# Batch 1's tokens in two transfers, states of batches 2 to 7 in two late groups, batch 3's tokens loaded ahead of batch 0's outputs

## The chip, the cores and the metric

The kernel runs on one core of a Trainium2 chip. The metric is the device time of one execution in microseconds (us). Engines are called as the profile calls them: PE is TensorE, DVE is VectorE, ACT is ScalarE, POOL is GpSimd and SP is SyncE, which here only issues DMAs.

## What is computed

The input has 8 batches of 8 heads, 512 tokens of 64 elements each, and 32 state vectors for each batch and head. Tokens attend to states, states attend to tokens, and the 544 resulting rows of each batch (heads side by side, 512 wide) go through a feed-forward layer with a leaky ReLU.

```python
def _attn_ref(x, state):
    B, H, S, D = x.shape                       # 8, 8, 512, 64; state: 8, 8, 32, 64
    scale = 1.0 / np.sqrt(D)
    a = softmax(scale * np.matmul(x, state.transpose(0, 1, 3, 2)))
    xread = np.matmul(a, state)
    a2 = softmax(scale * np.matmul(state, x.transpose(0, 1, 3, 2)))
    sread = np.matmul(a2, x)
    return np.concatenate([xread, sread], axis=2)

def _moe_ref(x, w_in, w_out):                  # 512x2048 and 2048x512
    h = x @ w_in
    return np.maximum(0.01 * h, h) @ w_out
```

(softmax stands for the reference's lines with maximum, exponential, sum and 1e-9.) Inputs and output are fp32; the kernel multiplies in bf16.

## The kernel before

Since xread @ w_in is a @ (state @ w_in), the kernel forms for each batch M = state @ w_in (`a_m`, in four column blocks c, evicted by `m_evict`) and the hidden layer directly from the probabilities and M (`ff1`, line 378, followed by ACT's Prelu, line 383). The second layer, FF2, is cut into pieces: `piece(b, hT, i, jq)` (line 406) is four matmuls for output tile i of batch b, and four pieces (jq 0 to 3) finish a tile, which `y_store` evicts and sends out through SP's queue.

For each batch the attention part is: tokens are loaded (`load_x`, into a ring of two tiles `xl`), cast to bf16 with heads side by side (`cast_x`, tile `xb`), and transposed, by PE (`a_xt_pe`, `a_xt_full`) or by a DMA on SP's queue (`a_xt_dma`, line 207), into `xT`. `a_scores` (line 236) makes the scores on PE. `a_shift` (three DVE instructions of 128x1024), `a_exp` (ACT) and `a_probs` (DVE) make the token-side probabilities `aT`. `a_max2` (DVE), `a_exp2` (ACT), `a_probs2` (DVE, lines 310 to 315) make the state-side probabilities `a2`; `a_a2t` (line 322) transposes them by a DMA on SP's queue, and `a_sread` (line 330) multiplies them with the tokens into `sr_t`, which a last stage for all states uses.

All orders are written out by hand: each engine runs its instructions in program order, and SP and POOL issue their DMAs in program order. Tile buffers come from rings; PSUM has two banks each for the tags `ph` and `py` and one double bank each for `sc` and `big`.

The prologue (to line 585) loads batch 0 on SP's queue, states of batches 0 and 1 on ACT's, and the weights and tokens of batches 1 and 2 on POOL's queue, with a cast for the weights. `spin` runs matmuls on zeros. The states of batches 2 and 3 come early, as `st2f`, and are turned on PE by `state23`. Then batch 0's hidden layer is made (lines 590 to 633), and from line 637 to 670 FF2 pieces of batch 0 run while batch 1's tokens are transposed and its attention made. Lines 674 to 711 are the hidden layer of batch 1 in 16 steps s, with FF2 pieces between and batch 2's attention; the states of batches 4 to 7 are loaded at step 6 by eight DMAs on SP's queue (`load_state`, line 187). The loop at line 716 does the same for batches 2 to 7: at step 1 of batch b the scores of batch b+1, at step 13 the token transposes of batch b+2; those tokens are loaded at step 0 (`load_x`) and cast by POOL at step 1. Batch 3's tokens are loaded at line 675, cast at line 691 and transposed at line 711. `state_t` (line 192) casts the late states on POOL and transposes them by a DMA on SP's queue.

Of the kernel before, what the change touches and what calls it, by code (L numbers as in the profile page):

```python
# [9 lines left out]
P = 128  # L10
B, H, S, D = 8, 8, 512, 64
NS = 32
# [3 lines left out]
NT = S // P  # L16
# [11 lines left out]
def kernel(  # L28
# [34 lines left out]
    xv = x[0].rearrange("h (p t) d -> p h (t d)", t=NT)  # L63
    for u in range(2):
        nc.sync.dma_start(xf[u][:], xv[:, NK * u:NK * (u + 1)])
    st2f = consts.tile([P, 4, D], FP32, name="st2f")
    nc.sync.dma_start(
        st2f[:], state[2:4].rearrange("b h n d -> (b h n) d").rearrange("(p r) d -> p r d", r=4)
    )
    idle = consts.tile([P, S], BF16, name="idle")  # L70
    nc.vector.memset(idle[:], 0.0)
    warm = consts.tile([P, 2], FP32, name="warm")
# [26 lines left out]
    def load_x(b, eng):  # L99
        xl[b] = xpool.tile([P, H, NT * D], FP32, name="xl", tag="xl", bufs=2)  # L100
        eng.dma_start(xl[b][:], x[b].rearrange("h (p t) d -> p h (t d)", t=NT))
# [4 lines left out]
    def cast_x(b, h0, h1, copy):  # L106
        copy(  # L107
            xs[b][:, :, h0:h1].rearrange("p t h d -> p h t d"),
            xl[b][:, h0:h1].rearrange("p h (t d) -> p h t d", t=NT),
        )  # L110
# [27 lines left out]

    stbd = consts.tile([P, NK, 2, NS], BF16, name="stbd")
    st1 = consts.tile([P, P], BF16, name="st1")  # L140
    st23 = consts.tile([P, 2, P], BF16, name="st23")
    st_t = consts.tile([P, B - 4, P], BF16, name="st_t")
    sr_t = consts.tile([P, NK, B * NS], BF16, name="sr_t")

    stb0 = consts.tile([P, 4, D], BF16, name="stb0")
# [15 lines left out]
            ps[:, :, D:].rearrange("p r (k q) -> p k q r", q=8),  # L161
        )

    stb2 = consts.tile([P, 4, D], BF16, name="stb2")

    def state23():
        ps = psum.tile([P, 4, D], FP32, name="pst2", tag="sc", bufs=1)
        for r in range(4):
            for g in range(2):
                nc.tensor.matmul(  # L170
                    ps[D * g:D * (g + 1), r, :].rearrange("p (c q) -> p c q", q=8),
                    lhsT=stb2[:, r, :],
                    rhs=ident[:].rearrange("p (c v q) -> p c v q", v=2, q=8)[:, :, g],
                    start=True, stop=True,
                )
        SCA(
            st23[:].rearrange("p b (k q r) -> p (b k) q r", k=NK, r=4),
            ps[:].rearrange("p r (c q) -> p c q r", q=8),
        )

    stf = consts.tile([P, B - 4, P], FP32, name="stf")
    stb = consts.tile([P, B - 4, P], BF16, name="stb")

    def load_state():
        for k in range(NK):
            for g in range(2):
                nc.sync.dma_start(
                    stf[NS * k:NS * (k + 1), :, D * g:D * (g + 1)],
                    state[4:, 2 * k + g].rearrange("b n d -> n b d"),
                )  # L190

    def state_t():
        POO(stb[:], stf[:])
        nc.sync.dma_start_transpose(st_t[:], stb[:].rearrange("p b q -> p (b q)"))

# [27 lines left out]
    def st_of(a, g, k):  # L225
        rows = slice(D * g, D * (g + 1))
        if a.b == 0:
            return stbd[rows, k, g ^ (k // 2), :]
        t = st1 if a.b == 1 else st23[:, a.b - 2] if a.b < 4 else st_t[:, a.b - 4]
        return t[rows, NS * k:NS * (k + 1)]  # L230

    def a_scores(a):
# [167 lines left out]
    def piece(b, hT, i, jq, bank=None, copy=SCA):  # L400
        if jq == 0:
            y = ys[b, i] = Y()
            y.py = psum.tile([P, DM], FP32, name="py", tag="py")[:] if bank is None else bank
        y = ys[b, i]
        for j in range(4 * jq, 4 * jq + 4):
            nc.tensor.matmul(  # L406
                y.py, lhsT=hT[:, j, P * i:P * (i + 1)], rhs=w_out_bf[:, j, :],
                start=(j == 0), stop=(j == 15),
            )
        if jq == 3 and copy is not None:  # L410
            y_store(b, i, copy)
# [138 lines left out]
        load_w_in(c)  # L550
    cast_x0(6, 8, POO)
    load_w_out(0)
    load_x(1, nc.gpsimd)
    for c in range(1, 4):
        load_w_out(c)
    load_x(2, nc.gpsimd)
# [4 lines left out]
    pxt = x0_half(1)  # L561
    m = max0(0)
    xt0_evict(1, pxt, (SCA, VEC))
    SCA(stb2[:], st2f[:])
    rows0(0)
    m = split0(m)
    scores0(1)
# [1 line left out]
    rows0(1)  # L569
    spread0(scn[0], m[0], False)  # L570
    exp0(0)
    state23()
    spread0(scn[1], split0(m[1]), False)
    exp0(1)
    sum0(0)
# [48 lines left out]
    for j, tag in ((4, "py"), (6, "sc"), (8, "py"), (10, "ph"), (12, "py"), (14, "ph")):  # L624
# [4 lines left out]
        if j == 8:  # L629
            m_evict(a0, 3, a_m(a0, 3, "big"), VEC)  # L630
            a_scores(a0)
            a_max2(a0)
    cast_x(1, 0, 4, VEC)
    cast_x(1, 4, 6, SCA)
    cast_x(1, 6, 8, POO)

    for g in range(2):
        a_exp2(a0, g)
    for i in (0, 1):
        piece(0, h0, i, 0)  # L640
    wide = psum.tile([P, 2, DM], FP32, name="pyw", tag="big", bufs=1)
    for i in (2, 3):
        piece(0, h0, i, 0, bank=wide[:, i - 2])
    for t0, copy in ((0, VEC), (2, SCA)):
        ps = psum.tile([P, 2, NK, P], BF16, name="pxt2", tag="ph")
        a_xt_pe(a1, ps, t0, t0 + 2)
        copy(a1.xT[:, t0:t0 + 2], ps[:])
    for i in range(NT):
        piece(0, h0, i, 1)
        if i == 0:  # L650
            a_scores(a1)
        if i < 3:
            m_evict(a1, 1 + i, a_m(a1, 1 + i, "ph"), SCA)
    a_shift(a1)
    a_max2(a1)
    a_exp(a1)
    for g in range(2):
        a_exp2(a1, g)
    a_probs(a1)
    open_xb(2)  # L660
    cast_x(2, 0, 8, SCA)
    for i in range(NT):
        piece(0, h0, i, 2)
    for i in (2, 3):
        piece(0, h0, i, 3, copy=None)
    for i in (2, 3):
        y_store(0, i, VEC)
    a_probs2(a0)
    a_a2t(a0)
    a_open(a2, 2)  # L670
# [1 line left out]


    h1 = hpool.tile([P, 16, S], BF16, name="hT", tag="hT")
    load_x(3, nc.sync)
    open_xb(3)
    fill = [(0, h0, 0, 3), (0, h0, 1, 3)] + [(1, h1, i, jq) for jq in range(3) for i in range(2)]
    for s in range(16):
        ff1(a1, h1, s)
        if s % 2:  # L680
            pb, hT, i, jq = fill[s // 2]
            piece(pb, hT, i, jq, copy=VEC if s == 3 else SCA)
        if s == 2:
            a_xt_full(a2)
            VEC(a2.xT[:], a2.pxt[:])
        elif s == 4:
            a_scores(a2)
            m_evict(a2, 0, a_m(a2, 0, "big"), SCA)
            a_shift(a2)
            a_max2(a2)  # L690
            cast_x(3, 0, 8, POO)
        elif s == 6:
            load_state()
        elif s == 8:
            a_exp(a2)
            a_probs2(a1)
            a_a2t(a1)
        elif s == 9:
            a_sread(a0)
        elif s == 10:  # L700
            a_exp2(a2, 0)
            a_probs(a2)
        elif s == 12:
            a_exp2(a2, 1)
            a_probs2(a2)
        elif s == 14:
            pm = [a_m(a2, 1, "big"), a_m(a2, 2, "sc")]
            m_evict(a2, 1, pm[0], VEC)
            m_evict(a2, 2, pm[1], SCA)
            a_open(att_of[3], 3)  # L710
            a_xt_dma(att_of[3])

# [1 line left out]
    for b in range(2, B):  # L716
        hT = hpool.tile([P, 16, S], BF16, name="hT", tag="hT")
        a = att_of[b]
        nxt = att_of[b + 1] if b + 1 < B else None
        order = [(b - 1, i, 3) for i in range(2)]  # L720
        order += [(b - 1, i, jq) for i in range(2, NT) for jq in range(4)]
        order += [(b, i, jq) for jq in range(3) for i in range(2)]
        for s in range(16):
            ff1(a, hT, s)
            if s == 0:
                if b + 2 < B:
                    load_x(b + 2, nc.sync)
                    open_xb(b + 2)
                a_a2t(a)
            elif s == 1:  # L730
                if nxt is not None:
                    a_scores(nxt)
                m_evict(a, 3, a_m(a, 3, "big"), SCA)
                if nxt is not None:
                    a_shift(nxt)
                    a_max2(nxt)
                if b + 2 < B:
                    cast_x(b + 2, 0, 8, POO)
            elif s == 4:
                if b == 2:  # L740
                    state_t()
            elif s == 6:
                if b == 2:
                    a_sread(a1)
            elif s == 8:
                a_sread(a)
            if nxt is not None:
                if s == 5:
                    a_exp(nxt)
                elif s in (6, 7):  # L750
                    a_exp2(nxt, s - 6)
                    if s == 7:
                        a_probs(nxt)
                        a_probs2(nxt)
                elif s == 10:
                    pm0 = a_m(nxt, 0, "big")
                    pm2 = a_m(nxt, 2, "phpy")
                    pm1 = a_m(nxt, 1, "sc")
                    m_evict(nxt, 2, pm2, VEC)
                    m_evict(nxt, 0, pm0, VEC)  # L760
                    m_evict(nxt, 1, pm1, SCA)
                if s == 13 and b + 2 < B:
                    a_open(att_of[b + 2], b + 2)
                    a_xt_dma(att_of[b + 2])
            pb, i, jq = order[s]
            piece(pb, hT if pb == b else h_prev, i, jq)
        h_prev = hT
# [48 lines left out]
```

## Time and profile before

| | |
|---|---|
| Median of three runs | 219.7 us (219.4 to 219.81) |
| The profiled execution's own time | 220.09 us |
| Its span, first to last instruction | 218.0 us |
| Granted TensorE clock | 1.000 throughout |
| PE busy | 209.7 us (96%) |
| ACT busy | 139.9 us (64%) |
| DVE busy | 100.2 us (46%) |
| POOL busy | 22.2 us (10%) |
| PE's first FF1 matmul of batch 1 | 38.05 us from the span's start |
| PE's first scores matmul of batch 3 | 58.02 us from the span's start |

All positions in time below count from the span's start. In rows of the timeline the first number is the start, the second the time covered by a run of equal instructions, and the square bracket gives the idle time of the engine before it and what ended that. A matmul's time includes its way through the array, so matmuls in a row overlap: four of 128x512 take about 0.86 us of PE. "SPq" rows are DMA issues by SP; the data land later.

### The profile page before, as it was taken

The numbers are of one execution on the slowest core, as the hardware profiler recorded it, in microseconds if no ns is written. First come the engines' busy times: TensorE is split into PE (matmuls) and PEld (weight loads), VectorE is DVE, ScalarE is ACT, GpSimd is POOL, SyncE is SP. The second block draws the span as 40 slices with busy tenths as digits, with TensorE's granted clock in tenths as the row PEclk, the third lists the DMA queues.
The fourth block names the chain that finished last, engine by engine and source line by source line (L and its number), as shares of the span: only waits on it lengthen the run. The fifth ranks groups of instructions, "written<-read, shape, count | busy, mean of one in ns | idle before, by whom it ended". The sixth has DMA issues, their size and how long they took to land.

```text
span 218.0 us, 3745 instructions
## 1 busy us (share of the span) xinstructions
PE 209.7 (96%) x1530; PEld 98.5 (45%) x1530; DVE 100.2 (46%) x151; ACT 139.9 (64%) x263; POOL 22.2 (10%) x36
## 2 busy tenths in 40 slices
PE   7789999999899999999999999999999999999993
PEld 2533534443345444544444444444444445466552
DVE  1768278799488409650867066714673000000000
ACT  3567768689768656974787477747785665454420
POOL 8830200003040011000300030000000000000000
PEclk9999999999999999999999999999999999999999
DMA  6999990699792782159213941181113111111113
GB/s 169 239 207 289 213 278 9 162 278 119 195 215 72 159 229 96 51 128 257 96 51 92 264 129 48 50 144 58 42 59 88 48 48 48 51 48 48 51 48 96
DMA packets 37008, 27.11 MB, mean 124 GB/s; under 512 B 21504, under 2 KB 32256, under 8 KB 36992
## 3 DMA queue, kind: packets, MB, share of 16 engines
q1 hardware_dynamic: 32080, 20.45, 35.5%
q0 software_dynamic: 4768, 6.29, 14.2%
q10 hardware_dynamic: 144, 0.13, 0.6%
q8 instruction: 12, 0.20, 0.4%
q14 instruction: 4, 0.03, 0.1%
HBM read 17.30 MB, written 8.91 MB: 120 GB/s over the span
## 4 chain that ended last, share of the span: by engine, by line
PE 82%; DMA 8%; DVE 4%; POOL 2%; ACT 1%; SPq 1%; issue 1%; POOLq 0%; ACTq 0%
PE py L406 47%; PE ph L378 20%; DMA w_in_bf<-in_moe_w_in_dram 5%; PE pm L357 4%; PE pyw L406 3%; PE ph L389 3%; DMA xT<-xb 3%; PE ph L601 2%; PE psr L330 1%; PE sc L236 1%; PE pxt L215 1%; DMA out_dram<-ysb 1%; POOL w_in_bf L120 1%; DVE mrow L246 1%; DVE mrowb L254 1%; DVE M L371 1%
## 5 line engine op out<-in xcount | busy, mean ns | idle before, releaser
L406 PE MATMUL py<-w_out_bf,hT 128*128 128x512 bf16 x464 | 118.9, 379 | 0.0
L383 ACT ACTIVATE hT<-ph 128x512 bf16<-128x512 f32 x112 | 67.0, 601 | 43.2 <-PE ph L378 43.2
L406 PEld LDWEIGHTS <-hT 128*128 128x128 bf16 x496 | 46.9, 98 | 57.4 <-issue 5.3
L378 PE MATMUL ph<-aT,M 128*128 128x512 bf16 x224 | 66.1, 379 | 0.3 <-ACT hT L383 0.3
L378 PEld LDWEIGHTS <-M 128*128 128x128 bf16 x224 | 21.6, 98 | 27.0 <-issue 1.6
L415 ACT COPY ysb<-py 128x512 f32<-128x512 f32 x30 | 17.6, 586 | 10.5 <-PE py L406 10.5
L246 DVE TRANSPOSE_TENSOR_REDUCE mrow<-sc 128x32 f32<-128x1024 f32 x7 | 8.8, 1250 | 33.5 <-PE sc L236 33.4
L437 DVE COPY ysh<-pyh 128x256 f32<-128x256 f32 x1 | 0.4, 425 | 47.7 <-PE pyh L432 47.7
L107 POOL CAST xb<-xl 128x2048 bf16<-128x2048 f32 (+1 forms) x6 | 10.7, 1781 | 103.0 <-DMA xl<-in_x_dram 87.3
L371 ACT CAST M<-pm 128x1024 bf16<-128x1024 f32 x13 | 13.2, 1012 | 1.7 <-PE pm L357 1.2
L268 DVE TRANSPOSE_TENSOR_REDUCE r<-e 128x32 f32<-128x1024 bf16 x7 | 8.7, 1244 | 9.0 <-ACT e L263 9.0
L371 DVE CAST M<-pm 128x1024 bf16<-128x1024 f32 x9 | 11.0, 1217 | 2.2 <-PE pm L357 2.2
L304 ACT ACTIVATE e<-sc,mcols 128x512 bf16<-128x512 f32 x16 | 11.1, 698 | 0.0
L369 DVE CAST M<-pm 128x512 bf16<-128x512 f32 x12 | 7.7, 685 | 6.3 <-PE pm L357 6.3
L296 DVE TENSOR_REDUCE mcol<-sc 128x2 f32<-128x1024 f32 x8 | 9.7, 1214 | 0.0
L393 ACT ACTIVATE hs<-ph 128x256 bf16<-128x256 f32 x16 | 6.0, 385 | 4.6 <-PE ph L389 4.4
L277 DVE STREAM_TRANSPOSE qb<-qh 128x1024 bf16<-128x1024 bf16 x7 | 8.7, 1245 | 0.2
L254 DVE STREAM_TRANSPOSE mrowb<-mrow 128x1024 f32<-128x1024 f32 x7 | 8.7, 1245 | 0.2
L256 DVE TENSOR_TENSOR sh<-sc,mrowb 128x1024 f32<-128x1024 f32 x7 | 8.6, 1225 | 0.2
L389 PE MATMUL ph<-sr_t,w_in_bf 128*128 128x256 bf16 x64 | 8.3, 273 | 0.0
L609 ACT ACTIVATE hT<-ph 128x512 bf16<-128x512 f32 x12 | 6.4, 597 | 2.8 <-PE ph L601 2.7
L406 PE MATMUL pyw<-w_out_bf,hT 128*128 128x512 bf16 x32 | 7.6, 380 | 0.0
(101 smaller groups left out, 158.7 us busy)
## 6 DMA issues: line engine op xcount, KB each, us to landing
out_dram<-ysb SPq DMA_DIRECT2D x31, 256.0 KB, 2.3
xl<-in_x_dram SPq DMA_DIRECT2D x5, 1024.0 KB, 6.7
w_in_bf<-in_moe_w_in_dram POOLq DMA_DIRECT2D x4, 512.0 KB, 9.8
w_out_bf<-in_moe_w_out_dram POOLq DMA_DIRECT2D x4, 512.0 KB, 17.7
xl<-in_x_dram POOLq DMA_DIRECT2D x2, 1024.0 KB, 18.6
xf<-in_x_dram SPq DMA_DIRECT2D x2, 512.0 KB, 5.3
out_dram<-ysb SPq DMA_DIRECT2D x8, 64.0 KB, 1.7
stf<-in_state_dram SPq DMA_DIRECT2D x8, 32.0 KB, 4.9
```

The lines of the kernel that those rows point to most:

```text
L107: copy(xs[b][:, :, h0:h1].rearrange("p t h d -> p h t d"), xl[b][:, h0:h1].rearrange("p h (t d) -> p h t d", t=NT),)
L246: nc.vector.tensor_reduce(out=m1[:], in_=flat.rearrange("p (c j) -> p c j", j=NS), axis=AX.X, op=ALU.max, apply_transpose=True,)
L254: nc.vector.transpose(m1b[:], m1[:, :, None].to_broadcast([P, n, NS]))
L296: nc.vector.tensor_reduce(out=m2[:], in_=a.sc[:], axis=AX.X, op=ALU.max, negate=True)
L304: nc.scalar.activation(out=a.e2[:, g], in_=a.sc[:, g, :], func=AF.Exp, bias=a.m2s[:, g:g + 1], scale=SCALE, accum_out=a.r2[:, g:g + 1],)
L357: nc.tensor.matmul(at[v][NS * r:NS * (r + 1)], lhsT=st_of(a, g, k), rhs=w_in_bf[D * g:D * (g + 1), k, DM * c:DM * (c + 1)], start=True, st ...
L371: copy(a.M[:, :, cols], pm[:])
L378: nc.tensor.matmul(ph[:], lhsT=a.M[:, g, P * j:P * (j + 1)], rhs=a.aT[:, g, :], start=(g == 0), stop=(g == 1),)
L383: nc.scalar.activation(out=hT[:, j, :], in_=ph[:], func=AF.Prelu, alpha=0.01)
L389: nc.tensor.matmul(ph[:, :n], lhsT=w_in_bf[:, k, P * j:P * (j + 1)], rhs=sr_t[:, k, :], start=(k == 0), stop=(k == NK - 1),)
L406: nc.tensor.matmul(y.py, lhsT=hT[:, j, P * i:P * (i + 1)], rhs=w_out_bf[:, j, :], start=(j == 0), stop=(j == 15),)
L415: copy(ysb[:], ys[b, i].py)
```

## The change

The early load of batches 2's and 3's states, its cast and its transposition on PE go; two idle matmuls stand in the place of the eight. The states of batches 2 to 7 are now loaded in two groups, (2, 3) and (4 to 7), each by eight DMAs on SP's queue, a POOL cast and a DMA transpose. The first group's loads write a tile that DVE sets to zero in two columns right after it has cast batch 1's tokens, so they start after that. The second group's loads stand at step 4 of batch 2, and its cast and transpose at step 8.

Batch 1's tokens come in two transfers of four heads, both still on POOL's queue and in the same place. DVE makes both casts (before: DVE, ACT and POOL one part each), PE transposes four heads at a time with an FF2 piece after each, and DVE makes both copies out of PSUM (before: DVE and ACT). Scores, M blocks and the token-side chain of batch 1 follow in another order among the pieces.

Batch 3's tokens are loaded right after the first group's transpose, ahead of the outputs of batch 0 on SP's queue, and cast by POOL; batch 2's cast is split between ACT and POOL. In the hidden layer of batch 1, batch 0's `a_sread` moves from step 9 to 6, `a_exp` of batch 2 and `a_a2t` of batch 1 from step 8 to 7, with batch 3's `a_xt_dma` right behind (before: step 14); `a_exp2` moves from steps 10 and 12 to 9 and 11, and two M blocks of batch 2 from step 14 to 13.

```diff
-    st2f = consts.tile([P, 4, D], FP32, name="st2f")
-    nc.sync.dma_start(
-        st2f[:], state[2:4].rearrange("b h n d -> (b h n) d").rearrange("(p r) d -> p r d", r=4)
-    )
...
-    st23 = consts.tile([P, 2, P], BF16, name="st23")
-    st_t = consts.tile([P, B - 4, P], BF16, name="st_t")
+    groups = ((2, 4), (4, 8))
+    st_t = [consts.tile([P, hi - lo, P], BF16, name=f"st_t{lo}") for lo, hi in groups]
...
+    stf = [consts.tile([P, hi - lo, P], FP32, name=f"stf{lo}") for lo, hi in groups]
+    stb = [consts.tile([P, hi - lo, P], BF16, name=f"stb{lo}") for lo, hi in groups]
+
+    def load_state(i):
+        lo, hi = groups[i]
         for k in range(NK):
             for g in range(2):
                 nc.sync.dma_start(
-                    stf[NS * k:NS * (k + 1), :, D * g:D * (g + 1)],
-                    state[4:, 2 * k + g].rearrange("b n d -> n b d"),
-                )
-
-    def state_t():
-        POO(stb[:], stf[:])
-        nc.sync.dma_start_transpose(st_t[:], stb[:].rearrange("p b q -> p (b q)"))
+                    stf[i][NS * k:NS * (k + 1), :, D * g:D * (g + 1)],
+                    state[lo:hi, 2 * k + g].rearrange("b n d -> n b d"),
+                )
+
+    def state_t(i):
+        POO(stb[i][:], stf[i][:])
+        nc.sync.dma_start_transpose(st_t[i][:], stb[i][:].rearrange("p b q -> p (b q)"))
...
-    load_x(1, nc.gpsimd)
+    x1 = [consts.tile([P, NK, 2 * P], FP32, name="x1", tag=f"x1{u}") for u in range(2)]
+    for u in range(2):
+        nc.gpsimd.dma_start(
+            x1[u][:], x[1, NK * u:NK * (u + 1)].rearrange("h (p t) d -> p h (t d)", t=NT)
+        )
...
-    SCA(stb2[:], st2f[:])
...
-    state23()
+    spin(2, "py")
...
-    cast_x(1, 0, 4, VEC)
-    cast_x(1, 4, 6, SCA)
-    cast_x(1, 6, 8, POO)
+    for u in range(2):
+        VEC(
+            a1.xb[:, :, NK * u:NK * (u + 1)].rearrange("p t h d -> p h t d"),
+            x1[u][:].rearrange("p h (t d) -> p h t d", t=NT),
+        )
+    nc.vector.memset(stf[0][:, 0, D - 1:D + 1], 0.0)
+    load_state(0)
 
     for g in range(2):
         a_exp2(a0, g)
     for i in (0, 1):
         piece(0, h0, i, 0)
     wide = psum.tile([P, 2, DM], FP32, name="pyw", tag="big", bufs=1)
-    for i in (2, 3):
-        piece(0, h0, i, 0, bank=wide[:, i - 2])
-    for t0, copy in ((0, VEC), (2, SCA)):
-        ps = psum.tile([P, 2, NK, P], BF16, name="pxt2", tag="ph")
-        a_xt_pe(a1, ps, t0, t0 + 2)
-        copy(a1.xT[:, t0:t0 + 2], ps[:])
-    for i in range(NT):
-        piece(0, h0, i, 1)
-        if i == 0:
-            a_scores(a1)
-        if i < 3:
-            m_evict(a1, 1 + i, a_m(a1, 1 + i, "ph"), SCA)
+    for u in range(2):
+        ps = psum.tile([P, NT, 2, P], BF16, name="pxt2", tag="ph")
+        for t in range(NT):
+            for v in range(2):
+                h = NK * u + 2 * v
+                nc.tensor.transpose(
+                    ps[:, t, v, :], a1.xb[:, t, h:h + 2, :].rearrange("p h d -> p (h d)"), ident[:]
+                )
+        VEC(a1.xT[:, :, 2 * u:2 * u + 2, :], ps[:])
+        piece(0, h0, 2 + u, 0, bank=wide[:, u])
+    a_scores(a1)
+    m_evict(a1, 1, a_m(a1, 1, "ph"), SCA)
     a_shift(a1)
     a_max2(a1)
+    for i in (0, 1):
+        piece(0, h0, i, 1)
+    m_evict(a1, 2, a_m(a1, 2, "ph"), SCA)
     a_exp(a1)
+    for i in (2, 3):
+        piece(0, h0, i, 1)
+    m_evict(a1, 3, a_m(a1, 3, "ph"), SCA)
     for g in range(2):
         a_exp2(a1, g)
+    state_t(0)
+    load_x(3, nc.sync)
+    open_xb(3)
+    open_xb(2)
+    cast_x(2, 0, 4, SCA)
+    cast_x(2, 4, 8, POO)
     a_probs(a1)
-    open_xb(2)
-    cast_x(2, 0, 8, SCA)
...
     for i in (2, 3):
         y_store(0, i, VEC)
+    cast_x(3, 0, 8, POO)
     a_probs2(a0)
     a_a2t(a0)
...
-    load_x(3, nc.sync)
-    open_xb(3)
...
-            cast_x(3, 0, 8, POO)
         elif s == 6:
-            load_state()
-        elif s == 8:
+            a_sread(a0)
+        elif s == 7:
             a_exp(a2)
             a_probs2(a1)
             a_a2t(a1)
-        elif s == 9:
-            a_sread(a0)
-        elif s == 10:
-            a_exp2(a2, 0)
-            a_probs(a2)
-        elif s == 12:
-            a_exp2(a2, 1)
-            a_probs2(a2)
-        elif s == 14:
+            a_open(att_of[3], 3)
+            a_xt_dma(att_of[3])
+        elif s in (9, 11):
+            a_exp2(a2, s // 2 - 4)
+            if s == 9:
+                a_probs(a2)
+            else:
+                a_probs2(a2)
+        elif s == 13:
             pm = [a_m(a2, 1, "big"), a_m(a2, 2, "sc")]
             m_evict(a2, 1, pm[0], VEC)
             m_evict(a2, 2, pm[1], SCA)
-            a_open(att_of[3], 3)
-            a_xt_dma(att_of[3])
...
             elif s == 4:
                 if b == 2:
-                    state_t()
+                    load_state(1)
...
             elif s == 8:
                 a_sread(a)
+                if b == 2:
+                    state_t(1)
```

More of the change, by code (lines that the diff above doesn't have):

```diff
@@ L162, in state01 @@
         )
[L164 to L174, printed above, removed]
-                )
[L176 to L184, printed above, removed]
+    stf = [consts.tile([P, hi - lo, P], FP32, name=f"stf{lo}") for lo, hi in groups]
+    stb = [consts.tile([P, hi - lo, P], BF16, name=f"stb{lo}") for lo, hi in groups]
+    def load_state(i):
+        lo, hi = groups[i]
         for k in range(NK):
@@ L228, in st_of @@
             return stbd[rows, k, g ^ (k // 2), :]
-        t = st1 if a.b == 1 else st23[:, a.b - 2] if a.b < 4 else st_t[:, a.b - 4]
+        t = st1 if a.b == 1 else st_t[0][:, a.b - 2] if a.b < 4 else st_t[1][:, a.b - 4]
         return t[rows, NS * k:NS * (k + 1)]
```

## The prediction

> **What bounds the kernel now.** I read the page's first part, then the list of who waited for whom on TensorE (PE), then the timeline around each wait.
>
> ```profile
> span 218.0 us, 3745 instructions
> PE 209.7 (96%) x1530; PEld 98.5 (45%) x1530; DVE 100.2 (46%) x151; ACT 139.9 (64%) x263; POOL 22.2 (10%) x36
> ```
>
> PE is busy 209.7 of 218.0 us. The change takes no matmul of weight away from it, so all it can win is PE's waiting. The list of waits (us in total, times, longest) holds these three that the change touches:
>
> ```profile
> PE sc L236 <- DMA xT<-xb: 1.0, 1, 1.0
> PE pm L357 <- DMA w_in_bf<-in_moe_w_in_dram: 0.6, 1, 0.6
> PE sc L236 <- ACT xT L647: 0.2, 1, 0.2
> ```
>
> The largest is batch 3's scores waiting for its transposed tokens. The timeline (start, us, engine) shows why they are late:
>
> ```profile
> 43.71 7.11 SPq L187 DMA_DIRECT2D stf<-in_state_dram  x8
> 49.23 1.98 POOL L107 CAST xb<-xl 128x2048 bf16<-128x2048 f32 x1 [24.03 <-DMA xl<-in_x_dram]
> 50.92 1.24 SPq L322 DMA_TRANSPOSE a2T<-a  x1
> 52.27 3.49 SPq L207 DMA_TRANSPOSE xT<-xb  x1
> 58.02 0.41 PE L236 MATMUL sc<-xT,st 64*32 64x512 bf16 x8 [1.01 <-DMA xT<-xb]
> ```
>
> Eight state loads hold SP until 50.82; only then come batch 1's a2T and, behind it, batch 3's xT, which lands at 57.98. Batch 1's input to a2T was ready on DVE at 49.45, and batch 3's tokens were cast at 51.21.
>
> **The change part by part.** Below, "early" means against the times of before.
>
> *Prologue.* Gone are st2f (128 KB), its ACT cast (0.41), eight matmuls (0.32) and their ACT eviction (0.37); two idle matmuls come in their place (three took 0.82, so two about 0.6 with the tail). The ACT work lay before an idle 1.18 us. The matmuls end near a DVE wait at 10.35, at most 0.1 late, and that is absorbed by the 0.60 that PE waits for w_in at 15.82; without that cover it costs 0.1. The st2f bytes ran on the same 16 DMA engines as w_in, whose busy share in the windows from 4 to 19 us is 1.07 to 1.26, so full. Batch 1's tokens move at about 381 GB/s there; 131 KB at that rate are 0.34 us. I take w_in, w_out and x all 0.3 early, inside the 0.60 wait: **-0.3** (ends: 0, if other traffic fills the hole, and -0.4). Nothing is late behind it up to 22.6: the next weights land at 17.9 for a use at 19.1, and DVE's M evictions follow PE.
>
> *Batch 1's tokens in two transfers.* POOL now issues eleven transfers in place of ten. Before, the tenth (x of batch 2) was held until 12.61 by a w_in landing; now the last quarter of w_out is tenth, and batch 2's x, eleventh, is held by the next w_in landing, 15.8. That costs nothing because the queue is backed up: batch 2's bytes run only from 29.4, where the rate in the windows rises from 207 to 307 GB/s. Were that cover gone, x would land 3.2 later.
>
> The first half should land midway between w_out's first quarter (20.5) and 24.03, at 22.2, the second at 24.0, both 0.3 early. DVE casts each (0.69): done at 24.4. PE finishes its first two pieces at 24.05, does eight transposes (half of 16 in 0.84, so 0.42), a piece (0.86), eight more from 25.4, a piece to 26.7. DVE's second xT copy starts 0.64 after the transposes' start, as at 26.07/26.71, takes 0.69, and ends near 26.75. Before, ACT took 1.01 for the second copy, and PE stood from 27.82 to 28.22:
>
> ```profile
> 27.16 1.01 ACT L647 COPY xT<-pxt 128x1024 bf16<-128x1024 bf16 x1 [1.16 <-PE pxt L215]
> 28.22 0.41 PE L236 MATMUL sc<-xT,st 64*32 64x512 bf16 x8 [0.24 <-ACT xT L647]
> 37.30 0.69 DVE L278 TENSOR_TENSOR aT<-e,qb 128x1024 bf16<-128x1024 bf16 x1
> 38.05 1.04 PE L378 MATMUL ph<-aT,M 128*128 128x512 bf16 x4
> ```
>
> Of that 0.40 some 0.1 stays: **-0.3** (ends 0 and -0.4). What is late next is aT, which at 37.99 met PE at 38.05. Now batch 1's scores come 1.4 early (26.85 against 28.22). DVE's chain: mrow 27.3, then 1.27+1.27+1.23 to 31.1, mcol and mcols to 32.5, then the 3.85 that ran from 34.14 to 37.99: aT at 36.4. PE is there at 37.45. A second-half landing 0.8 later would still be hidden.
>
> *States of batches 2 and 3.* A two-column memset of DVE, queued behind the second cast, holds eight loads on SP until 24.5. Their issue row is 0.31 to 0.87, median 0.46; at 0.43 to 0.55 apiece SP is through at 28 to 29. Landing of such a load was 1.7 to 7.0 after issue, so the last lands between 29.7 and 36; I take 30.5 to 33.5, since no 1 MB load stands ahead of them on SP's queue as it did there. Then come POOL's cast of 256 columns (0.61 for 512: 0.4), the transpose's issue (1.2), and the load of batch 3's x at 32.5 to 35, against 41.91. The states are wanted at 42.3; the transpose landed 2.4 after issue, so 6 us are spare. Batch 3's x landed 6.0 to 7.3 after issue in all five SP rows: 38.5 to 42. SP's outputs and a2T of batch 0 stand behind all this, and they are not ready before 38.3.
>
> *First FF1 stage of batch 1 (38 to 57).* The sread of batch 0 (16 matmuls 0.47, two ACT copies 0.52) moves from step 9 to 6. It needs a2T, issued at 40.45 and landed 3.3 later, 43.75; PE comes at 45.2: no wait, 1.4 spare. The exponential moves from step 8 to 7; its input is ready at 47.2, so ACT stands some 0.2, and steps 8 and 9's Prelus (each 0.54 in a row) end at 48.8 and 49.3, with PE at step 10 at 48.7: 0.15 lost. The exp2's then sit at steps 9 and 11, one Prelu earlier than before, and the wait of 0.30 that PE had at 51.44 goes; I follow the queue to step 15 at 54.7 against 55.1, less 0.1 to 0.2 for the M cast that now stands ahead of step 14's Prelu. **-0.2** (ends -0.4 and +0.5, a Prelu's length).
>
> *Batch 3's xT.* No state loads stand ahead: a2T of batch 1 goes at 49.5 and xT 1.35 behind it, 50.85, 1.42 before the old 52.27. xT landed 5.7 after issue here and 4.4 to 4.5 later, so 55.3 to 56.6. PE is ready at 56.9, or 56.7 with the term above. Both sides shift alike with the earlier gains, since a2T waits on DVE's chain, which starts from PE's scores. **-1.1** (58.02 less 56.9; ends 0 and -1.1).
>
> *The rest.* The four late batches' states (eight loads, 0.61 cast, one transpose) move past outputs to steps 4 and 8 of batch 2, landing near 70; they are first used at 81. The output stores behind them have four buffers. x of batch 4 goes earlier by as much as xT. Cost 0; if the states came 10 us late it would be 1 for 1.
>
> *A price I can't exclude* is POOL's cast of batch 3's tokens, which now moves from 49.2 to about 39 to 42. Two DVE instructions on small tiles ran long beside such casts (first a row of the timeline, then the views of two lines: count, shortest, median and longest ns):
>
> ```profile
> 50.64 0.60 DVE L272 TENSOR_SCALAR r<-r 128x32 f32<-128x32 f32 x1
> L272 DVE TENSOR_SCALAR r<-r x7: 180/182/598, 35.4 to 158.2; 128x32 f32<-128x32 f32 x7
> L298 DVE TENSOR_SCALAR mcols<-mcol x8: 168/169/1122, 22.0 to 154.8; 128x2 f32<-128x2 f32 x8
> ```
>
> Both ended within 0.03 us of POOL's end (51.24 against 51.21; 64.58 against 64.55). So such a DVE instruction waits for the whole rest of a 1.9 us cast. At 38.8 to 39.8 in the new time DVE does the same kind (L310, L315) for batch 0's a2. DVE then has 0.9 before batch 2's xT copy and 0.1 more behind it, so the loss is between 0 and 0.9; a cast that starts at 37.9 or sooner, or after 39.8, costs nothing. I take **+0.2**, about the share of 38.5 to 42 that hits.
>
> The Trainium skill has a rule that speaks against the change here: the page "SBUF — State Buffer", section "Who interferes with whom", says that VectorE and GpSimd share one pair of SBUF ports, which the first to start locks for its whole instruction, and that copies from PSUM and reductions stay outside. The two rows above agree. By the rule a certain hit would make the sum -1.0 in place of -1.7.
>
> **Sum.** -0.3 -0.3 -0.2 -1.1 +0.2 = -1.7 against the profiled execution's own 220.09 (218.0 of span and 2.09 around it): 218.4. That execution lies 0.39 above the median of the three runs, 219.7, so on the median's scale 218.0. All terms at their best give -2.2, at their worst +1.4.
>
> **Rivals.**
>
> *The lock hits in full.* Batch 3's cast starts at 38.5 to 39.7, a2 of batch 0 comes 1.6 to 1.9 late, batch 2's chain 0.6 to 0.9 late, and with it batch 3's a2T and xT order. For it: x's estimate straddles that place. Against: 39.8 and later is as likely. Time 218.6 to 219.2.
>
> *The change doesn't do what it says.* xT of batch 3 is still late, since it stands behind a2T of batch 1, which waits on DVE until 49.45 however soon the tokens are there. If xT takes 5.7 and its issue stays near 52, the 1.1 remains: 219.0 to 219.4. Against it: SP was busy with states right up to 50.82.
>
> *Slower: the state loads starve.* SP runs in order: batch 2 and 3's transpose, the load of x, the outputs and batch 0's a2T all stand behind the landing of the eight loads, which start amid POOL's backlog (6.29 MB in its queue). From a landing at 37 on, x goes out just ahead of a2T, and behind an x load a2T took 6.1 to 7.0 (three rows) in place of 3.3: 46.9 against sread's 44.6, 2.3 of PE; each us more adds one. At 38 that is 3.0 less 1.7: 221.0. Against it: at the start SP's two x halves and st2f landed by 7.3 amid the w_in stream, so that queue is not starved; and the backlog ends at 34.3.
>
> **How the numbers follow.** Forecast 217.4 to 218.6: 0.56. Lock in full 0.16, no earlier xT 0.08, both faster. Bad ends that add up to within 0.2% (0.44 us, about what a measurement of this kernel can tell from no change): 0.08. Slower 0.12: starved states, or step 7's and 8's ACT order at its worst. The range 217.4 to 219.4 holds the first three, 0.80.
>
> **What would show it.** Right: no DMA wait on sc at L236's line in batch 3; xT of batch 3 issued near 50 and landed before 56; w_in's wait 0.3; scores of batch 1 near 26.9; POOL's batch 3 cast before 44. Wrong: a PE wait on a2T at sread, a DVE tensor_scalar of about 2 us near 39, the state loads landing after 37, or new waits of PE on Prelu at steps 10 to 13 above 0.5 in all.

## The result and the profile after

The changed kernel takes 217.59 us (median of four runs, 217.15 to 217.8); the kernel before, run beside it, 219.69 (219.4 to 219.81). The ratio is 0.9904, 95% interval 0.9883 to 0.9924: 2.1 us faster. The forecast was 218.0, range 217.4 to 219.4. The profiled execution took 217.8.

The page and TensorE's (PE's) list of waits (us in total, times, longest):

```profile
span 215.5 us, 3750 instructions
PE 208.9 (97%) x1524; PEld 98.2 (46%) x1524; DVE 100.2 (47%) x154; ACT 136.7 (63%) x259; POOL 22.9 (11%) x38
...
PE psr L311 <- DMA a2T<-a: 1.0, 1, 1.0
```

The spans differ by 2.5. The wait of batch 3's scores for xT is no longer on the list; a new wait of the same size is: `a_sread` of batch 0 (now line 311) for a2T. The timeline shows both:

```profile
33.76 0.40 POOL L174 CAST stb<-stf 128x256 bf16<-128x256 f32 x1 [17.82 <-DMA stf<-in_state_dram]
...
35.52 0.58 SPq L98 DMA_DIRECT2D xl<-in_x_dram  x1
...
38.57 2.14 SPq L303 DMA_TRANSPOSE a2T<-a  x1
...
41.80 1.90 POOL L104 CAST xb<-xl 128x2048 bf16<-128x2048 f32 x1 [6.65 <-DMA xl<-in_x_dram]
...
44.47 0.64 PE L311 MATMUL psr<-a2T,xb 128*128 128x64 bf16 x16 [1.01 <-DMA a2T<-a]
...
48.88 2.01 SPq L188 DMA_TRANSPOSE xT<-xb  x1
...
55.63 0.41 PE L217 MATMUL sc<-xT,st_t 64*32 64x512 bf16 x8
```

Batch 3's tokens leave SP at 35.52, a2T of batch 0 at 38.57. In the kernel before, that a2T landed 3.3 after its issue; here 5.9 (44.47 less 38.57), and PE stands 1.01.

To see where the time went I cut the span at three PE instructions: P0, FF2's first piece; P1, the first FF1 matmul of batch 1 (38.05 before); P3, batch 3's first scores matmul (58.02 before). Behind P3 every kernel here takes 159.84 to 160.01, but for e2 (160.34). All in us from the profiles; "a2T" is issue to use of batch 0's a2T where PE waits for it, else issue to landing:

| kernel | P0 | P0 to P1 | P1 to P3 | a2T, PE's wait | span |
|---|---|---|---|---|---|
| before | 22.61 | 15.44 | 19.97 | 3.3, 0 | 218.0 |
| after | 21.59 | 14.53 | 19.51 | 5.9, 1.01 | 215.5 |
| c1_after_again | 21.85 | 14.53 | 20.03 | 6.1, 1.54 | 216.3 |
| c2_after_again | 22.09 | 14.53 | 18.49 | 4.8, 0 | 215.0 |

So in the first pair of profiles -1.02 comes from the prologue, -0.91 from batch 0's FF2 stretch and only -0.46 from the stretch that the change was mostly about. The two later executions of the same kernel show that the first and the third of these are not constants.

### The profile page after: what moved, and what is told of

It reads as the page before. It is cut to its first block, busy times and chain, and to the rows that moved or that the text cites. A ratio compares the mean times of both kernels' runs of the same rounds, so it can differ in the third digit from the quotient of the medians.

```text
span 215.5 us, 3750 instructions
## 1 busy us (share of the span) xinstructions
PE 208.9 (97%) x1524; PEld 98.2 (46%) x1524; DVE 100.2 (47%) x154; ACT 136.7 (63%) x259; POOL 22.9 (11%) x38
## 4 chain that ended last, share of the span: by engine, by line
PE 90%; DMA 6%; DVE 1%; ACT 1%; SPq 1%; issue 0%; ACTq 0%
PE py L387 50%; PE ph L359 22%; PE pm L338 4%; PE pyw L387 3%; PE ph L370 3%; DMA a2T<-a 3%; PE ph L585 2%; DMA xf<-in_x_dram 2%; PE psr L311 2%; PE sc L217 1%; PE php L585 1%; DMA out_dram<-ysb 1%; PE pxth L441 1%; DVE M L352 1%; SPq L400 1%; PE scn L477 0%
## 5 line engine op out<-in xcount | busy, mean ns | idle before, releaser
L338 PE MATMUL pm<-w_in_bf,st_t 64*32 64x512 bf16 x192 | 7.6, 379 | 0.0
```

Of the source, the lines that this page charges most:

```text
L338: nc.tensor.matmul(at[v][NS * r:NS * (r + 1)], lhsT=st_of(a, g, k), rhs=w_in_bf[D * g:D * (g + 1), k, DM * c:DM * (c + 1)], start=True, st ...
```

## Experiments

Each kernel is the changed one with the edit shown, unless it says otherwise. Ratios are to the kernel before on the same chip.

**c1 and c2: the changed kernel again.** No edit.

> The changed kernel itself, once more beside the variants: 217.6, between 217.2 and 217.9 if the chip agrees with the first four runs. In its profile: psr waits about 1.0 us for a2T, and w_in's third quarter lands between 14.7 and 15.3 (three kernels without st2f had 14.8 to 15.2, three with it 15.3 to 15.8).

> The changed kernel once more, beside the run above on the same chip: 217.3 to 218.0; its wait of psr on a2T between 1.0 and 1.6 us, as in the two profiles so far.

c1: 217.88 us (216.92 to 218.57), ratio 0.9925 [0.9903, 0.9947]. c2: 217.88 (217.28 to 218.71), 0.9936 [0.9919, 0.9953]. The executions of one kernel spread over 1.8 us. The timelines of c1 and then c2 show what differs:

```profile
36.52 0.57 SPq L98 DMA_DIRECT2D xl<-in_x_dram  x1
39.10 1.44 SPq L303 DMA_TRANSPOSE a2T<-a  x1
...
45.26 0.64 PE L311 MATMUL psr<-a2T,xb 128*128 128x64 bf16 x16 [1.54 <-DMA a2T<-a]
```

```profile
35.69 0.57 SPq L98 DMA_DIRECT2D xl<-in_x_dram  x1
39.06 1.86 SPq L303 DMA_TRANSPOSE a2T<-a  x1
...
43.86 0.64 PE L311 MATMUL psr<-a2T,xb 128*128 128x64 bf16 x16
```

In c2 the load left 0.8 sooner than in c1 at the same a2T issue, and a2T took 4.8 in place of 6.1: no wait. P0 also moves between executions (21.59 to 22.09) with the landing of the weights: it comes 6.79 to 6.80 after PE's first use of w_in's third quarter, at 14.80, 15.06 and 15.29 in the three.

**e1: `a_sread` two steps later**, so that a late a2T is covered.

```diff
-        elif s == 6:
-            a_sread(a0)
+        elif s == 8:
+            a_sread(a0)
```

> The changed kernel with batch 0's sread at step 8 in place of step 6, nothing else. Theory A: in the changed kernel PE stands 1.18 us at sread (ready at 43.29, psr at 44.47) only because a2T of batch 0 lands 5.9 us after issue; two steps and a piece later PE comes at about 45.0, after the landing at 44.44, and the wait goes: 217.6 less 0.9 to 1.2, 216.4 to 216.7. Rival B: the wait hid ACT's new order; with PE 1.2 earlier at steps 8 to 13 the exponential (input ready at 45.3) and the exp2's make PE wait for Prelus, 0.3 to 0.9 of it comes back: 216.9 to 217.3, with PE waits on ACT's Prelu at L359 in the profile. Rival C: xT of batch 3 becomes the wait (landing 53.3, scores then at 54.5): no wait expected, but if it lands later than 54.5 the gain ends there.

217.92 us, ratio 0.9913 [0.99, 0.9925]. The wait on a2T is gone, and the time is not better. In its timeline ScalarE (ACT) pays instead: the exponential at step 7 stands for its input, the copies of `sr_t` queue behind it, and PE then waits for Prelu.

```profile
45.67 1.06 ACT L244 ACTIVATE e<-sh 128x1024 bf16<-128x1024 f32 x1 [0.72 <-DVE sh L237]
...
47.11 0.52 ACT L318 CAST sr_t<-psr 64x128 bf16<-64x128 f32 x2
...
48.30 0.59 PE L359 MATMUL ph<-aT,M 128*128 128x512 bf16 x2 [0.45 <-ACT hT L364]
```

P1 to P3 is 19.03, against 18.49 in c2: 0.54 for having the copies behind the exponential. At step 6, in c2, the copies end at 45.07 and the exponential starts at 45.80, so there they stand ahead of it.

**e7: the old order of ACT's work** in batch 1's FF1 stage; **e8: the same with `a_sread` at step 7.**

```diff
-        elif s == 6:
-            a_sread(a0)
         elif s == 7:
-            a_exp(a2)
             a_probs2(a1); a_a2t(a1); a_open(att_of[3], 3); a_xt_dma(att_of[3])
-        elif s in (9, 11):
+        elif s == 8:
+            a_exp(a2)
+        elif s == 9:            # e8: at step 7, ahead of the rest
+            a_sread(a0)
+        elif s in (10, 12):
```

> The changed kernel with steps 6 to 12 in the old order: exponential of batch 2 at step 8, sread at 9, the exp2's at 10 and 12; batch 1's a2T and batch 3's xT stay at step 7. Theory A: in the run with sread at step 8 the exponential at step 7 held ACT until its input came (45.6) and with it the Prelus, for 0.7 of PE's time; behind step 8's Prelu it costs what it cost before, 0.3: 217.0 to 217.2, with a wait on ACT of 0.3 in place of 0.4 to 0.7. Rival B: the Prelus wait wherever the exponential stands, since ACT is full between 43 and 53: 217.6 to 217.9, as with sread at step 8.

> The run with steps 6 to 12 in the old order, but batch 0's sread at step 7 in place of 9, so that its two ACT copies fall into the 0.66 that ACT stood idle before step 8's Prelu there. Theory A (ACT's order sets these waits): PE's wait of 0.30 on a Prelu at step 13 goes; from the first FF1 of batch 1 to batch 3's scores 18.6 us in place of 18.9 (changed kernel 19.5 and 20.0): 217.3 to 217.5. Rival B: at step 7 PE comes 8.5 us after its first FF1, and a2T landed 7.2 to 8.8 after it in four runs, so PE waits up to 0.3 again: 217.6 to 217.8, with psr waiting on a2T.

e7: 217.68 us (217.54 to 217.77), 0.9913 [0.9898, 0.9928]; P1 to P3 18.89. e8: 217.91, 0.9919 [0.9906, 0.9932]; P1 to P3 19.32. The old order has one wait on Prelu, the 0.30 that the kernel before had too, and is 0.40 longer than c2's 18.49. But its sread, three steps later, didn't wait for a2T in the profile, and its runs lie within 0.23 us of each other. In e8 a2T landed 6.3 after issue, so the copies came late all the same. First e7's, then e8's timeline:

```profile
50.02 0.59 PE L359 MATMUL ph<-aT,M 128*128 128x512 bf16 x2 [0.30 <-ACT hT L364]
```

```profile
46.12 0.53 ACT L318 CAST sr_t<-psr 64x128 bf16<-64x128 f32 x2 [1.00 <-PE psr L311]
...
48.76 0.59 PE L359 MATMUL ph<-aT,M 128*128 128x512 bf16 x2 [0.52 <-ACT hT L364]
```

**e5: batch 3's tokens loaded sooner**, right behind the eight state loads on SP; **e6: later**, behind batch 0's a2T.

```diff
-    load_x(2, nc.gpsimd)           # e5
...
     load_state(0)
+    load_x(2, nc.gpsimd)           # e5
+    load_x(3, nc.sync)             # e5
...
-    load_x(3, nc.sync)             # e5 and e6
...
     a_a2t(a0)
+    load_x(3, nc.sync)             # e6, with cast_x(3, 0, 8, POO) behind it
```

In e5 the line of batch 2's load moves down too, but POOL's order of transfers stays, and the load goes out at 15.50 (15.04 in after).

> The changed kernel with batch 3's tokens loaded right behind the eight state loads on SP's queue, ahead of the states' transpose: issued near 27.1 in place of 35.5. Theory A: a2T of batch 0 lands late (5.9 us after issue) because the 1 MB load stands in front of it on the same queue; with the load gone by then a2T lands 3.3 to 4 after its issue near 38.6, before PE's sread at 43.3, and the wait of 1.2 goes; as in the run with sread at step 8 some 0.7 of it comes back as waits on ACT's Prelus: 217.1 to 217.3. Rival B: the load now shares the DMA engines with the last w_out and batch 2's tokens, which land near 36.5 in place of 33.9; batch 2's transposes (38.3) still have them, but above 37.2 PE waits there one for one. Rival C: POOL's cast of batch 3 then falls beside batch 0's a2 on DVE (37.5 to 38.5) and the lock costs up to 0.9; a DVE tensor_scalar of 1 us or more would show it.

> The changed kernel with batch 3's tokens loaded behind batch 0's a2T on SP's queue (about 39.9 to 40.8 in place of 35.5): the part 'fetched sooner' taken back but for 1 us. Theory A (the queue): a2T lands 3.3 after its issue near 38.6, sread does not wait; the tokens land near 47, POOL casts them to 49, xT is issued near 49.2 and lands near 53.7, before PE's scores at 54.5: the same gain as with the load first, 217.1 to 217.3, and the earlier fetch was worth nothing beyond SP's free queue. Rival B: the tokens now set the end: xT is issued after 50, lands after 55, and PE waits for it: 217.6 or more, with a DMA wait on xT at L217. Rival C: a2T is slow for another cause (the two outputs ahead of it): it still lands 5 to 6 after issue, 217.6.

e5: 217.66 us, 0.9914 [0.9897, 0.9931]. e6: 218.2, 0.9945 [0.9928, 0.9961]. In both a2T landed 3.1 after its issue and sread didn't wait, so it is the load shortly ahead on SP's queue that makes a2T slow. But in both POOL's cast of batch 3's tokens now fell on VectorE (DVE) instructions of a2, those of batch 0 in e5 and of batch 1 in e6. Their timelines, e5 first:

```profile
37.78 1.89 POOL L104 CAST xb<-xl 128x2048 bf16<-128x2048 f32 x1 [1.64 <-DMA xl<-in_x_dram]
37.99 1.70 DVE L291 TENSOR_SCALAR r<-r 128x2 f32<-128x2 f32 x1
...
49.62 2.02 SPq L188 DMA_TRANSPOSE xT<-xb  x1
...
55.85 0.41 PE L217 MATMUL sc<-xT,st_t 64*32 64x512 bf16 x8 [0.45 <-DMA xT<-xb]
```

```profile
46.47 1.93 POOL L104 CAST xb<-xl 128x2048 bf16<-128x2048 f32 x1 [11.58 <-DMA xl<-in_x_dram]
46.87 1.93 DVE L296 TENSOR_SCALAR a<-e,qc 128x512 bf16<-128x512 bf16 x2
...
50.16 1.80 SPq L188 DMA_TRANSPOSE xT<-xb  x1
...
55.51 0.41 PE L217 MATMUL sc<-xT,st_t 64*32 64x512 bf16 x8 [0.87 <-DMA xT<-xb]
```

An instruction on 128x2 takes 1.70, where a free one took 0.16, and the pair on 128x512 takes 1.93, free 0.62. In e6 the delay runs on through a2T to xT, which goes out 14.07 behind P1 in place of c2's 12.76 and lands 5.3 after that, and PE waits 0.87 at batch 3's scores. In e5 idle time of DVE takes most of the delay up: xT goes out 12.88 behind P1, 0.12 later than in c2. Its wait of 0.45 comes with an xT that landed 6.2 after issue, where c2's took 4.9; e3's xT, issued later still (49.88), took 4.8, and PE didn't wait. What made e5's transfer slow stays open.

**e3: batch 1's M blocks among single pieces**, as before the change.

```diff
-    for i in (0, 1):
-        piece(0, h0, i, 1)
+    piece(0, h0, 0, 1)
     m_evict(a1, 2, a_m(a1, 2, "ph"), SCA)
+    piece(0, h0, 1, 1)
+    m_evict(a1, 3, a_m(a1, 3, "ph"), SCA)
     a_exp(a1)
...
-    m_evict(a1, 3, a_m(a1, 3, "ph"), SCA)
```

> The changed kernel with the M blocks of batch 1 after one FF2 piece each, as before (one piece between blocks 1, 2 and 3, then two pieces), with the exponential behind the third block. Theory A: the two ph banks that a block takes are freed by ACT's copies of the block before, 1.07 us for two; after one piece (0.86) PE waits about 0.28 for the second bank, twice: +0.56, 218.2, and each block takes 0.6 to 0.7 again in the timeline (0.33 in the changed kernel, 0.61 before). Rival B: those gaps are the price of switching shapes and not of the banks: no change, 217.6. Rival C: the later exponential delays aT beyond PE's arrival and adds to it: above 218.4, with PE's first FF1 of batch 1 waiting on aT.

217.97 us, 0.9918 [0.9903, 0.9933]. P0 to P1 is 15.10 in place of 14.53, +0.57. Batch 1's M blocks in the timelines of before (with the weight load that stands inside one), after, and e3 (with ACT's eviction of the block ahead and the weight load):

```profile
29.75 0.69 PE L357 MATMUL pm<-w_in_bf,st 64*32 64x512 bf16 x8
30.03 0.11 PEld L357 LDWEIGHTS <-st 64*32 64x32 bf16 x6 [0.19 <-issue]
```

```profile
28.42 0.41 PE L338 MATMUL pm<-w_in_bf,st 64*32 64x512 bf16 x8
```

```profile
27.15 1.07 ACT L350 CAST M<-pm 128x512 bf16<-128x512 f32 x2 [2.61 <-PE pm L338]
...
27.99 0.69 PE L338 MATMUL pm<-w_in_bf,st 64*32 64x512 bf16 x8
28.28 0.11 PEld L338 LDWEIGHTS <-st 64*32 64x32 bf16 x6 [0.20 <-issue]
...
29.58 0.69 PE L338 MATMUL pm<-w_in_bf,st 64*32 64x512 bf16 x8
```

Eight matmuls of a block take 0.41, but 0.69 when the block follows the last one within a single piece: its second `ph` bank has not yet been evicted by ACT. In e3 ACT's two copies end at 28.22, and the rest of the block goes on at 28.28. A change of shape alone is not the price, since after's block stands behind FF2 pieces too and takes 0.41. Two such blocks make 2 x 0.28 = 0.56. The profile puts this down as "issue" of PEld, not as a wait of PE for ACT. The whole time rose by little, because everything behind P1 came later while the load on SP didn't, and a2T, 4.4 after its issue at 39.56, met no waiting PE (P1 to P3 18.48).

**e4: the kernel before with late states later only.** `load_state` goes from step 6 of batch 1 to step 4 of batch 2, `state_t` from step 4 to step 8 of batch 2; the other parts of the change are left out.

> The kernel before with one part of the change alone: the states of batches 4 to 7 loaded at step 4 of batch 2 and cast and transposed at step 8, in place of step 6 of batch 1 and step 4 of batch 2. Theory A: SP's eight state loads alone kept batch 3's xT late; a2T of batch 1 then goes at 49.5, xT when POOL's cast ends at 51.2, and lands at 55.7 to 57.0 against PE's 56.9: 1.0 to 1.1 less than before, 218.6. Rival B: without the earlier load of batch 3's tokens xT stays late; of the 1.1 at least 0.7 remains: 219.3 or more.

219.18 us, 0.9966 [0.9954, 0.9978]. Half of the wait for xT goes. In its timeline SP is free at once, but the tokens' cast ends only at 51.0:

```profile
48.95 2.05 POOL L107 CAST xb<-xl 128x2048 bf16<-128x2048 f32 x1 [23.61 <-DMA xl<-in_x_dram]
51.02 1.84 SPq L207 DMA_TRANSPOSE xT<-xb  x1
...
57.29 0.41 PE L236 MATMUL sc<-xT,st 64*32 64x512 bf16 x8 [0.49 <-DMA xT<-xb]
```

Of the wait of 1.01 that PE had here, 0.49 is left. That the earlier tokens are the other half is not shown: xT left 13.19 behind P1, 0.43 later than in after, but it also took 6.2 to land in place of 4.4, and with 4.4 it would have been there before PE.

**e2: the bytes of st2f put back**, as a load of the same 128 KB in the same place behind batch 0's tokens on SP, into a tile that is overwritten later.

```diff
+    nc.sync.dma_start(
+        stf[1][:, 0:2].rearrange("p b (r d) -> p (b r) d", d=D),
+        state[2:4].rearrange("b h n d -> (b h n) d").rearrange("(p r) d -> p r d", r=4),
+    )
```

> The changed kernel with one load more: the 128 KB of states of batches 2 and 3 in st2f's old form and place on SP's queue, into a tile that nobody reads before it is overwritten; so its output is unchanged. It prices st2f alone. Theory A (mine, from its bytes): 0.34 us of the 16 DMA engines, so w_in's third quarter lands 0.3 later and the time is 217.9. Theory B: st2f accounts for all of the 1.0 us by which PE's wait on w_in ended sooner (15.82 against 14.80): 218.6. Theory C: that 1.0 is a difference between two executions, not the load: 217.6, third quarter still near 14.8.

219.32 us (218.21 to 219.45), 0.9956 [0.9937, 0.9975]. Its P0 is 22.14. The three profiles with these bytes (before, e4, e2) have P0 at 22.61, 22.40 and 22.14, mean 22.38; the eleven without, 21.56 to 22.21, mean 21.96. So by the means the change of the prologue is worth about 0.42, and the rest of the 1.02 between the first two profiles is spread. The bytes alone are not settled: before and e4 also have st2f's cast, its matmuls and batch 1's tokens in one load, and e2, which adds the bytes alone, lies 0.18 above the mean without them and inside their spread. What stays open is why e2's time rose by 0.2 to 0.5% by the ratios. Its profiled span of 217.1 also holds a wait of 1.37 for a2T (6.4 after issue), 0.22 between P0 and P1, and 0.45 in the last output store. The 0.22 is POOL's cast of batch 2's second half beside DVE's product for aT:

```profile
35.25 1.04 POOL L104 CAST xb<-xl 128x1024 bf16<-128x1024 f32 x1
35.25 1.58 DVE L264 TENSOR_TENSOR aT<-e,qb 128x1024 bf16<-128x1024 bf16 x1
```

aT ends at 36.83 and FF1 starts at 36.89. In e5 the same product took 1.52, and P0 to P1 0.16 longer. In both the states landed late (cast from 34.75 and 34.90 on), and that cast stands behind theirs. In c1, where it stands as late but DVE's product came first, it was the cast that took longer (1.50), and P0 to P1 stayed at 14.53. Neither this nor the other two parts is traced to the bytes.

**e10 and e11: the load out of a2T's way.** In e10 both a2T's go ahead of the load. In e11 the load stands between them, and DVE makes the cast, so POOL can hold nothing up.

```diff
     a_probs2(a0); a_a2t(a0)
-    # load_x(3) ahead of the outputs, cast_x(3, 0, 8, POO) ahead of a_probs2(a0)
+    a_probs2(a1); a_a2t(a1); load_x(3, nc.sync); cast_x(3, 0, 8, POO)   # e10
+    load_x(3, nc.sync); a_probs2(a1); a_a2t(a1)                         # e11
...
         elif s == 7:
             a_exp(a2)
-            a_probs2(a1); a_a2t(a1)
+            cast_x(3, 0, 8, VEC)                                        # e11
             a_open(att_of[3], 3)
             a_xt_dma(att_of[3])
```

> The changed kernel with batch 1's a2 made right behind batch 0's on DVE (1.0 us, into the 0.84 that DVE stands idle before batch 2's xT copy), both a2T's behind each other on SP, and batch 3's tokens loaded behind them (about 41). Theory A, from the runs so far: batch 0's a2T, with no load ahead, lands 3.1 to 3.3 after issue, sread at step 6 does not wait; POOL's cast of batch 3 falls at 47.4 to 49.3, where DVE has no a2 any more, so the lock hits only a small operation of batch 2's token side, which has 1.5 to spare; xT of batch 3 is issued near 49.4, lands near 54 against PE's 54.6. From first FF1 of batch 1 to batch 3's scores 18.5 us, as in the run with single pieces, against 19.5 and 20.0: 216.6 to 216.9. Rival B: DVE is 0.2 late with batch 2's xT copy and the chain behind it makes ACT's exponential late: 0.2 to 0.5 of it lost, 217.1. Rival C: xT lands after 54.6, since the cast or the load is later than reckoned: one for one, 217.0 to 217.6, with a DMA wait at L217.

> Batch 1's a2 right behind batch 0's on DVE as in the run before, but batch 3's tokens loaded between the two a2T's (about 39.8) and cast by DVE behind batch 2's max2, in place of POOL; so POOL's lock has nothing to hold in this stage. DVE's fp32 cast of 128x1024 took 0.69, so 128x2048 about 1.4 against POOL's 1.9. Theory A: a2T of batch 0 lands 3.1 to 3.3 after issue, no wait at sread; tokens land near 46.5, are cast by 48.0, xT is issued at 48.1 and lands at 52.5 to 54.3, before PE's 54.6; from first FF1 of batch 1 to batch 3's scores 18.5 (changed kernel 19.5 and 20.0): 216.5 to 216.9. Rival B: batch 2's token side, 1.4 later on DVE behind the cast, makes PE wait for aT at batch 2's first FF1 (wanted 17.7 after batch 1's first, aT reckoned at 16.1): one for one beyond 17.7. Rival C: the tokens land after 47.5, and xT is again late: 217.2 or more.

e10: 218.3 us, 0.9934 [0.9922, 0.9947]. No wait at sread, but PE now waits 0.98 for xT. The cast of the later tokens sends xT out 13.30 behind P1, 0.54 later than in c2, and it landed 6.2 after issue in place of 4.9; with 4.9 PE would not have waited. The timeline:

```profile
48.13 1.89 POOL L104 CAST xb<-xl 128x2048 bf16<-128x2048 f32 x1 [12.61 <-PE ph L359]
50.05 1.78 SPq L188 DMA_TRANSPOSE xT<-xb  x1
...
56.28 0.41 PE L217 MATMUL sc<-xT,st_t 64*32 64x512 bf16 x8 [0.98 <-DMA xT<-xb]
```

e11: 216.96 us (216.85 to 217.1), ratio 0.988 [0.9867, 0.9893], faster than both kernels: its interval lies below that of c2, which ran on the same chip. Its timeline has no wait at either place:

```profile
43.75 0.63 PE L311 MATMUL psr<-a2T,xb 128*128 128x64 bf16 x16
...
46.96 1.22 DVE L104 CAST xb<-xl 128x2048 bf16<-128x2048 f32 x1
48.24 1.80 SPq L188 DMA_TRANSPOSE xT<-xb  x1
...
55.06 0.41 PE L217 MATMUL sc<-xT,st_t 64*32 64x512 bf16 x8
```

P1 to P3 is 18.48, as in c2's profile, and batch 0's a2T landed 3.2 after issue. Batch 1's a2T, now 0.67 behind the load, took 6.4, but its sread comes much later. The runs span 0.25 us where c2's span 1.43.

## Why the forecast held, and which steps did not

The time came out 0.4 below the forecast, and that it came so near is in part luck. Measured, the terms without a wait at sread add up to -2.8 (-0.4 -0.9 -0.4 -1.1, and 0 for the lock) against the forecast's -1.7; a wait for a2T that the forecast had at nothing, 0 to 1.54, gives part of it back. Two slips in the working left the forecast as it was: with all terms at their best the sum is -2.3, not -2.2, and the third rival's 3.0 is 3.3 by its own steps.

*Batch 3's xT, -1.1: right.* From batch 2's first FF1 matmul to P3 the profiles show 2.90 before (55.12 to 58.02) and 1.82 after (53.81 to 55.63): -1.08. e4 shows that moving the states alone takes away half of PE's wait; what the earlier tokens add is not shown.

*ACT's order, -0.2: right in sign.* Where sread doesn't wait (c2, e3, e11), P1 to P3 is 1.48 shorter than before; less the 1.08 that leaves -0.40, the best end of this term. e7 shows the same 0.40 by putting the order back.

*sread, "no wait, 1.4 spare": the step that failed.* I took a2T's 3.3 from the old place on SP's queue, where no load of tokens stood ahead of it. The mechanism is that of my rival, a2T slowed by an x load, but I let it begin only when the states land at 37 or later. They had landed by 33.76, just past the forecast's 33.5, the load left 3.05 before a2T, and that was not enough: 5.9, and 1.01 of PE. Without the load shortly ahead (e5, e6, e10, e11) a2T takes 3.1 to 3.2. How late a2T is goes with the landing of the load, as the eight profiles with load and a2T in the changed kernel's places show (us; the last column is the difference of the two landings):

| kernel | load ahead of a2T by | load lands | a2T's issue to landing | a2T lands behind the load by |
|---|---|---|---|---|
| e3 | 3.99 | 41.5 | 4.4 | 2.5 |
| e7 | 3.49 | 41.3 | 4.7 | 2.5 |
| e1 | 3.45 | 41.3 | 4.6 | 2.2 |
| c2 | 3.37 | 41.1 | 4.8 | 2.8 |
| after | 3.05 | 41.7 | 5.9 | 2.8 |
| e8 | 2.83 | 43.2 | 6.3 | 2.2 |
| c1 | 2.58 | 42.7 | 6.1 | 2.5 |
| e2 | 2.47 | 43.4 | 6.4 | 2.2 |

The load takes 5.4 to 6.9, and a2T lands 2.2 to 2.8 behind it whatever the lead. The size of that gap belongs to this place: batch 2's a2T, issued 0.6 to 2.8 behind the load of batch 4's tokens, landed 0.8 to 0.9 behind it in all fourteen profiles. PE comes for batch 0's at 43.5 (after) to 43.9 (c2), so with the load landed at 41.1 (c2) there is no wait, at 42.7 (c1) it is 1.54. My price, an a2T that is free of the load as soon as the two are not issued in a row, had no row behind it.

*Batch 1's scores, -0.3: mis-sized, measured -0.91.* The waits for xT that I counted are there (0.34 of it, by difference). I left out that the new order also spaces the M blocks: 0.57, which e3 gives back exactly. The cause stood in the trace of before as rows of 0.69 beside rows of 0.41, not in its list of waits, from which I had chosen what to cost.

*Prologue, -0.3: right in size, its cause open.* -0.42 by the means; a single pair of profiles would have said -1.02. That it is the bytes, as I reckoned, is not shown: e2's P0 moved by 0.18, inside the spread, while its time leaves a larger cost open.

*POOL's lock, +0.2: the mechanism is right, and the cast missed DVE's a2 here.* It came at 41.80 (41.16 and 42.81 in c2 and c1), later than DVE's a2 instructions. e5 and e6 move it onto them: in e6 PE waits 0.87, inside the end of 0.9, though xT's landing 5.3 after issue, not c2's 4.9, is a part of it; in e5, on batch 0's a2 as in the first rival, no more than 0.12 of delay reached xT's issue. I looked only at batch 3's cast; the one that cost PE 0.16 (e5) and 0.22 (e2) is that of batch 2's second half beside aT. The Trainium skill's rule on the shared port, which the forecast cited (page "SBUF — State Buffer", section "Who interferes with whom"), agrees with these rows (0.16 against 1.70 for the same instruction).

The first rival (the lock in full) failed on the cast's time, the second (xT still late) on the issue at 48.88. The third did happen, in its mechanism, and took up to 1.5 of the gain without turning its sign. In c1 the states landed a microsecond later than in after (34.78), and the load left at 36.52 in place of 35.52.

## What to carry to other kernels

A DMA transpose that PE will soon need should not be issued while a large load ahead of it on the same queue is still under way: reckon its landing from the load's landing (0.8 to 2.8 behind it here), and place the load behind it where a later use allows that, as in e11. A stall in the middle of a matmul group has to be read from the rows' lengths (0.69 beside 0.41), since the list of waits doesn't name it. And before a gain is put down to a term, the same kernel's profile should be taken more than once: here one stretch alone moved by 1.5 us between executions.

## What the runs showed of the hardware that I had not expected

- A DMA transpose behind one 128x2048 fp32 load on SP's queue landed after that load in all these profiles, by 2.2 to 2.8 us (batch 0's a2T, even when it was issued 4 us behind the load) or by 0.8 to 0.9 (batch 2's); with no such load under way ahead of it batch 0's takes 3.1 to 3.3.
- POOL's cast holds up not only DVE instructions on tiny tiles. Beside a cast DVE's product aT<-e,qb, 0.69 us in the trace of before, took longer: 1.58 in e2's timeline above, and after's shows 0.99.

```profile
34.11 1.04 POOL L104 CAST xb<-xl 128x1024 bf16<-128x1024 f32 x1
34.70 0.99 DVE L259 TENSOR_TENSOR aT<-e,qb 128x1024 bf16<-128x1024 bf16 x1
```

- The same cast of 128x2048 from fp32 to bf16 takes 1.22 on DVE (e11) and 1.89 to 1.93 on POOL (e10, e6).
